# Last products of eight half groups by seven block products in an mLSTM cell with a multiplicative FFN

## The chip, the cores and the metric

The kernel runs on one core of a Trainium2 chip. A core has four computing engines that run side by side, each through its own queue of instructions: TensorE (PE in the profile; its weight loads are PEld), VectorE (DVE), ScalarE (ACT) and GpSimd (POOL). SyncE (SP) issues most DMAs, and ACT issues those of the output. [...]VectorE and ScalarE read PSUM, GpSimd works on SBUF.

The metric is the device time of one execution in microseconds (us); lower is better. All data are fp32.

## The reference

An mLSTM cell runs over 768 positions of 4 batches with 8 heads of 40. Its output, as 3072 tokens of 320 values, goes through a feed-forward block:

```python
for t in range(S):                                   # cell, per batch and head
    m_new = max(f_gate[t] + m, i_gate[t])
    f_stab, i_stab = exp(f_gate[t] + m - m_new), exp(i_gate[t] - m_new)
    C = f_stab * C + i_stab * outer(v[t], k[t])
    n = f_stab * n + i_stab * k[t]
    y[t] = sigmoid(o_gate[t]) * (C @ q[t]) / max(|n . q[t]|, 1)
x = y.transpose(0, 2, 1, 3).reshape(3072, 320)
a, b = x @ w1, x @ w2                                # 320 x 1024 each
out = ((a * b) @ w3) @ w_out                         # 1024 x 1024, 1024 x 320
```

## The kernel before

The two last weights are first multiplied into one, `w3o` (1024 x 320, eight blocks of 128 rows), so that out = (a * b) @ w3o. What is left is a cell and two products: the *up* products, which give a and b, and the *last* products.

**Steps.** One loop over 32 steps, `s` = 0 to 31 (L820), holds everything. The cell is cut into 24 pieces (`NU`) of one batch and 128 positions. Step `s` sends piece `s` through its first half (scores, state) and piece `s - 1` through its second half (`h`, denominators, `y`): this is "the cell's work", `quarter_work` (L338). Its PSUM is two tiles, `cell[0]` and `cell[1]`, of two banks each: `cell[0]` holds scores and state updates, `cell[1]` the two parts of `h`. The other four banks come from `mps` in turn. After step 24 the cell's banks are given to `mps` as well.

Four pieces of the same positions, one for each batch, make a group `gr` of 512 tokens; there are six. A half group `(gr, j)` has 256 tokens. `y` goes through DRAM (`send`, `get_back`) and comes back to be turned by VectorE (`x_turn`, L468), two steps after its piece.

**Up products.** Groups 0 to 2 use ordinary products (`up`), in steps up to 15. Groups 3 to 5 go by Strassen's scheme in Winograd's form, seven block products for eight (`up_by_seven`, L668), one eighth of a group's features each in steps 19 to 30. Its four parts are called in this order: `single` (three products into `pa` and `pb`, four `mps` banks), `shared` (four products for each of a and b into the cell's banks up to step 24: `p15` in `cell[1]`, copied out by ACT at L702 and L704, `p67` in `cell[0]`, added by VectorE at L684 and L686, then two adds by GpSimd at L711), `left` (the rest of the features on TensorE, and four adds that read `pa`, `pb` and the results of L711: "the left adds") and `product` (a * b on GpSimd, L729). The sums of tokens that the scheme needs are made by `token_sums` (L661), at the end of steps 17, 21 and 25.

**Last products.** Up to step 24 they are plain: `ffn_out` (L733) multiplies one block of 128 tokens with `w3o` in eight matmuls of 320 columns, into the cell's banks; ACT copies the result out and issues the DMA. `downs` lists 14 blocks, groups 0 to 2 and the first half of group 3; `n_down` says how many a step takes: two in steps 16 to 20, one in steps 21 to 24.

The five half groups from (3, 1) on go by seven (`out_by_seven`, L772), each 28 matmuls of 160 columns, at steps 27, 29 and three at step 31 (`n_out`). They need four sums of quarters of `w3o` (`out_weight_sums`, L748: one at step 24 and three at step 25, on GpSimd) and four sums of quarters of a * b (`ab_sums`, L763: on VectorE). In what follows A11 to A22 are the quarters of a half group of a * b, S1 to S4 their sums, B11 to B22 the quarters of `w3o`, T1 to T4 their sums.

**Order.** TensorE's instructions keep the order in which the program has them (`in_order`, L84), and so do those of every other engine (`keep_order`, L549, called in the last step for the whole loop, L979). Between the engines semaphores are set where data or memory ask for it. In a step the order is: `single` and `shared`, the last products, `left`, the cell's work; then, with GpSimd first, `product`, sums of output weights, `ab_sums` (at step 25 here, else at the end of the block), `x_turn`, the transposes of the next keys and queries (`turn`), `token_sums`; then `weighted`, `weights`, `masks` for the next piece (GpSimd L330, ACT L303, GpSimd L308), and the loads of later pieces. After step 24, `single` comes behind the last products.

Of the kernel before, what the change touches and what calls it, by code (L numbers as in the profile page):

```python
# [8 lines left out]
FP = mybir.dt.float32  # L9
U32 = mybir.dt.uint32  # L10
AF = mybir.ActivationFunctionType
OP = mybir.AluOpType
# [4 lines left out]
def kernel(  # L17
# [49 lines left out]
    io = ctx.enter_context(tc.tile_pool(name="io", bufs=3))  # L67
# [23 lines left out]
    def mm(out, lhsT, rhs, start=True, stop=True):  # L91
        in_order(nc.tensor.matmul(out, lhsT=lhsT, rhs=rhs, start=start, stop=stop))  # L92
# [134 lines left out]
        pend.append((dst, raw_tile(dst.shape[-1] if dst is not None else CW, pieces), i, part))  # L227


    w3T_t = {}  # L230
    turned_w3, ready_w3 = [], []

# [4 lines left out]
    def convert():  # L237
        if not scaled:
            scale_next()
        dst, raw, ko, half = scaled.pop(0)  # L240
        if dst is not None:
            to_f32(dst, raw)
            return
        w3 = wst.tile([128, CW], FP, name="w3", tag="w3")
        to_f32(w3, raw)
        if half == 0:
            w3T_t[ko] = wst.tile([128, FO, 128], FP, name="w3T", tag="w3T")
        nc.vector.transpose(out=w3T_t[ko].rearrange("c k (m r) -> c m k r", r=32)[:, 2 * half:2 * half + 2],
                            in_=w3.rearrange("r (m c k) -> r m k c", m=2, k=FO))
        if half:  # L250
            turned_w3.append(ko)
# [495 lines left out]

    def out_weight_sums():  # L748

        T_o.extend(m[:, i * KH * NH:(i + 1) * KH * NH].rearrange("p (f n) -> p f n", n=NH)  # L750
                   for m, i in ((v_all, 0), (gates, 0), (gates, 1), (q_all, 0)))
        (B11, B12), (B21, B22) = ([w3o[:, k * KH:(k + 1) * KH, i * NH:(i + 1) * NH] for i in range(2)] for k in range(2))
        T1, T2, T3, T4 = T_o
        for dst, p, q in ((T1, B12, B11), (T2, B22, T1), (T3, B22, B12), (T4, B21, T2)):
            yield nc.gpsimd.tensor_tensor(out=dst, in0=p, in1=q, op=OP.subtract)

    T_o, S_o = [], {}
    wsums = out_weight_sums()

    def quarters_of_ab(gr, j):  # L760
        return [[ab_t[gr][j][:, k * KH:(k + 1) * KH, t * P:(t + 1) * P] for k in range(2)] for t in range(2)]

    def ab_sums(gr, j):  # L763
        mem = [t.rearrange("p h d -> p (h d)") if j == 0 else io.tile([P, H, L], FP, name="pw", tag="pw", bufs=5)
               .rearrange("p h t -> p (h t)") for t in kbuf]
# [6 lines left out]
    def out_by_seven(gr, j, sums=None):  # L772
# [6 lines left out]
        o2 = (v_all, q_all)[j][:, 2 * DM:4 * DM].rearrange("p (i n) -> p i n", n=NH)  # L779

        def products(pairs, name):
            po = mps([P, len(pairs), NH], name)
            for i, (a, b) in enumerate(pairs):
                for f in range(KH):
                    mm(po[:, i], a[:, f, :], b[:, f, :], start=(i == f == 0), stop=(i == len(pairs) - 1 and f == KH - 1))
            return po
# [6 lines left out]
        for i in range(2):  # L793
            nc.vector.tensor_tensor(out=o2[:, 1 + i], in0=p67[:, i], in1=o2[:, i], op=OP.add)
        nc.vector.tensor_tensor(out=o2[:, 1:4:2], in0=o2[:, 1:3], in1=o2[:, 3:4].to_broadcast([P, 2, NH]), op=OP.add)
        nc.vector.tensor_tensor(out=o2[:, 0:2], in0=p23, in1=o2[:, 0:2], op=OP.add)
        nc.vector.tensor_tensor(out=o2[:, 2:3], in0=p4, in1=o2[:, 2:3], op=OP.add)
# [6 lines left out]
    downs = [(gr, j) for gr in range(NG) for j in range(GT)][:14]  # L804
    outs = [(gr, j) for gr in range(3, NG) for j in range(2)][1:]
# [14 lines left out]
    for s in range(len(n_up)):  # L820
# [33 lines left out]
            ab_sums(*summed.pop(0))  # L854
        def pairs():
            for i in range(n_out[s]):
                out_by_seven(*outs.pop(0))
                if summed and n_out[s] > 1:
                    ab_sums(*summed.pop(0))

        seven = None
        if s == NU + 3:
            pairs()
        if n_seven[s]:
            seven = up_by_seven(*sevens.pop(0), (lambda i: cell[i // 2][:, i % 2].rearrange("p (i t) -> p i t", i=2)) if s <= NU else
                                lambda i: mps([128, 2, TH], "p67" if i < 2 else "p15"), nc.gpsimd if sevens else nc.vector)
# [5 lines left out]
        else:  # L872
            for _ in range(n_down[s]):
                ffn_out([downs.pop(0)])
        if s != NU + 3:
            pairs()
        if seven and s > NU:
            seven[0]()
        now = [ups.pop(0) for _ in range(n_up[s])]
# [132 lines left out]
```

## Time and profile before

| | us |
|---|---|
| three runs | 426.82, 427.91, 428.42 |
| median | 427.91 |
| the profiled execution's own time | 427.89 |
| its span in the trace | 425.84 |
| steps 21 to 23, each | 14.13 |
| from the end of the cell (335.03) to the end of TensorE's work (about 422.6) | 87.6 |

The span runs from the first instruction to the last; some 2 us of the execution lie around it. The granted TensorE clock was 0.996 of full speed over the whole span, and full in every stretch from 240 us on.

A busy time in the profile is a sum of durations. A matmul's duration includes the time in which it runs beside the next, so its cost is better read from the distance of two starts: the 56 instructions of a half group by seven take 7.61 from the first to the start of what follows, 0.136 each. One fp32 product stands as two instructions in the trace.

A bracket at the end of a timeline line says how long the engine sat idle before the line and what ended this.

### The profile page before, as it was taken

What the parts mean: (1) busy time and instruction counts of PE and PEld (TensorE: products, weight loads), DVE (VectorE), ACT (ScalarE), POOL (GpSimd) and SP (SyncE); (2) the same over time, 40 slices, a digit from 0 to 9 for tenths busy, and PEclk for the clock granted to TensorE, in tenths of its full rate; (3) what the DMA queues carried; (4) which work ended last, traced back from release to release, by engine and by line L of the source; (5) the groups of instructions that cost most, each with busy time, mean ns of one, the idle gap of its engine ahead of it and who ended that gap; (6) DMA issues with size and microseconds to landing.
All of it is one profiled execution on the core that took longest, in us unless ns stands there. A gap on an engine that the chain in (4) does not pass through costs nothing.

```text
span 425.8 us, 13079 instructions
## 1 busy us (share of the span) xinstructions
PE 414.1 (97%) x5353; PEld 335.3 (79%) x5353; DVE 313.5 (74%) x635; ACT 150.1 (35%) x404; POOL 154.3 (36%) x211
## 2 busy tenths in 40 slices
PE   7989989999999999999999999999999999999996
PEld 4768878888688788787777778788778879888896
DVE  6676986888949779778736966596868699575971
ACT  4766865567723623630433313032311110210000
POOL 4421342233303303303307751546453587542100
PEclk9989999999999999999999999999999999999999
DMA  8999998598977776985425675756421120000001
GB/s 186 204 173 245 214 144 140 134 193 180 215 183 154 166 182 135 181 164 105 89 80 130 153 141 121 142 133 117 87 44 36 35 39 2 31 2 31 2 32 62
DMA packets 135211, 51.15 MB, mean 120 GB/s; under 512 B 109360, under 2 KB 126960, under 8 KB 135152
## 3 DMA queue, kind: packets, MB, share of 16 engines
q1 hardware_dynamic: 131552, 46.29, 53.9%
q10 hardware_dynamic: 3600, 4.03, 2.7%
q8 instruction: 42, 0.69, 0.7%
q14 instruction: 17, 0.14, 0.1%
HBM read 44.50 MB, written 5.80 MB: 118 GB/s over the span
## 4 chain that ended last, share of the span: by engine, by line
PE 53%; issue 20%; DVE 7%; POOL 7%; SPq 7%; DMA 5%; ACT 1%; POOLq 0%; DVEq 0%
PE cell L92 17%; PE pa L92 12%; PE o L92 8%; PE pb L92 8%; PE p L92 3%; POOL pw L308 3%; SPq L184 3%; DVE w3T L666 2%; PE pt L95 1%; POOL vw L330 1%; SPq L148 1%; DMA raw<-in_moe_w_dram 1%; PE fill L92 1%; POOL raw L659 1%; POOL state L335 1%
## 5 line engine op out<-in xcount | busy, mean ns | idle before, releaser
L335 POOL TENSOR_TENSOR state<-state,decay 128x164 f32<-128x164 f32 x40 | 20.0, 500 | 154.8 <-DVE state L404 129.0
L92 PE MATMUL pa<-xT,w 128*128 128x256 f32 x240 | 60.4, 382 | 0.0
L92 PEld LDWEIGHTS pa<-xT,w 128*128 128x128 f32 x240 | 44.4, 190 | 6.8 <-DVE h L430 0.4
L303 ACT ACTIVATE pw<-pw,aT 128x64 f32<-128x64 f32 x184 | 46.4, 339 | 3.2 <-ACT o_sb L741 1.9
L92 PE MATMUL pb<-xT,w 128*128 128x256 f32 x192 | 45.4, 379 | 0.0
L729 POOL TENSOR_TENSOR ab<-ab,a_sb 128x512 f32<-128x512 f32 x22 | 29.4, 1356 | 32.2 <-DVE ab L684 32.2
L92 PEld LDWEIGHTS pb<-xT,w 128*128 128x128 f32 x192 | 36.4, 190 | 5.0
L711 POOL TENSOR_TENSOR wo<-wo 128x512 f32<-128x512 f32 x22 | 27.4, 1268 | 29.8 <-DVE wo L686 29.8
L92 PE MATMUL pa<-xT,wr 64*64 64x256 f32 x384 | 37.0, 386 | 0.5 <-DVE wr L200 0.5
L92 PE MATMUL wp<-wo,w3T 128*128 128x320 f32 x128 | 35.9, 433 | 1.1 <-DVE ab L639 0.6
L308 POOL TENSOR_SCALAR_AFFINE_SELECT pw<-pw 64x512 f32<-64x512 f32 x48 | 35.8, 746 | 3.0 <-ACT pw L303 1.2
L92 PE MATMUL pb<-xT,wr 64*64 64x256 f32 x384 | 36.4, 380 | 0.0
L92 PE MATMUL cell<-w3o,ab 128*128 128x320 f32 x128 | 35.4, 432 | 0.0
L638 ACT ACTIVATE a_sb<-pa 128x512 f32<-128x512 f32 x24 | 14.3, 598 | 59.0 <-PE pb L92 59.0
L639 DVE TENSOR_TENSOR ab<-pb,a_sb 128x512 f32<-128x512 f32 x24 | 16.4, 688 | 23.2 <-ACT a_sb L638 22.8
L92 PEld LDWEIGHTS wp<-wo,w3T 128*128 128x128 f32 x128 | 23.8, 190 | 10.5 <-DVE ab L639 0.8
L92 PEld LDWEIGHTS cell<-w3o,ab 128*128 128x128 f32 x128 | 24.3, 190 | 9.5
L92 PEld LDWEIGHTS pa<-xT,wr 64*64 64x64 f32 x384 | 18.9, 132 | 15.4 <-issue 8.8
L686 DVE SCALAR_TENSOR_TENSOR a_sb<-pa,wo 128x512 f32<-128x512 f32 x12 | 8.3, 689 | 29.8 <-PE pa L92 29.8
L430 DVE TENSOR_TENSOR h<-cell,h 64x164 f32<-64x164 f32 x88 | 28.6, 326 | 1.6
L92 PE MATMUL po<-w3o,ab 128*128 128x320 f32 x96 | 26.4, 433 | 0.0
L92 PEld LDWEIGHTS po<-w3o,ab 128*128 128x128 f32 x96 | 18.1, 190 | 7.3
(180 smaller groups left out, 846.4 us busy)
## 6 DMA issues: line engine op xcount, KB each, us to landing
raw<-in_moe_w_dram SPq DMA_DIRECT2D x64, 128.0 KB, 3.4
kbuf<-in_k_dram SPq DMA_DIRECT2D x24, 160.0 KB, 4.5
v_all<-in_v_dram SPq DMA_DIRECT2D x24, 160.0 KB, 4.9
o_in<-in_o_gate_dram SPq DMA_DIRECT2D x24, 160.0 KB, 4.8
pw<-U_d SPq DMA_DIRECT2D x28, 128.0 KB, 3.5
raw<-in_moe_w_dram SPq DMA_DIRECT2D x5, 512.0 KB, 6.7
raw<-in_moe_w_out_dram SPq DMA_DIRECT2D x8, 320.0 KB, 4.1
gates<-in_k_dram SPq DMA_DIRECT2D x28, 80.0 KB, 2.5
```

Source lines behind the costliest of these rows:

```text
L92: in_order(nc.tensor.matmul(out, lhsT=lhsT, rhs=rhs, start=start, stop=stop))
L184: nc.sync.dma_start(out=dst, in_=src)
L303: nc.scalar.activation(out=pw[:, h, :], in_=src[:, h, :], func=AF.Exp, bias=aT[:, c, b * H + h:b * H + h + 1])
L308: nc.gpsimd.affine_select(out=pw[r], in_=pw[r], compare_op=OP.is_ge, fill=0.0, base=0, pattern=[[0, H], [1, L]], channel_multiplier=-1)
L335: nc.gpsimd.tensor_tensor(out=new, in0=old, op=OP.mult, in1=decay[:, b * NP:(b + 1) * NP, 2 * c + x:2 * c + x + 1] .to_broadcast([P, NP, D1]))
L430: nc.vector.tensor_tensor(out=part, in0=ph[x][halves[e]], in1=part, op=OP.add)
L638: nc.scalar.mul(out=a_sb, in_=pa, mul=UP ** -2)
L639: nc.vector.tensor_tensor(out=ab_t[gr][j][:, fs[0]:fs[-1] + 1, t0:t0 + a_sb.shape[-1]], in0=pb, in1=a_sb, op=OP.mult)
L666: nc.vector.tensor_tensor(out=dst, in0=p, in1=q, op=OP.subtract)
L686: nc.vector.scalar_tensor_tensor(out=out, in0=p, scalar=UP ** -2, in1=q, op0=OP.mult, op1=OP.add)
L711: aside_by.tensor_tensor(out=kept[j][:, 1:4:2], in0=kept[j][:, 1:3], in1=kept[j][:, 3:4].to_broadcast([128, 2, TH]), op=OP.add)
L729: aside_by.tensor_tensor(out=t[:, f:FO:FH, :], in0=t[:, f:FO:FH, :], in1=a, op=OP.mult)
```

## The change

- The last products of all half groups from (2, 0) on, eight in place of five, go by seven. The six blocks of group 2 and the first half of group 3 leave `downs`. `n_out` puts one half group into each of steps 21, 22, 24, 26 and 28, and three into step 31; `n_down` takes two blocks in steps 16 to 18 and one in steps 19 and 20.
- Up to step 24 the seven products go into the cell's four banks: `o15` and `o23` into `cell[1]`, `o67` and `o4` into `cell[0]`. Later they use `mps`, as before.
- The order of the products is A11 B11, A12 B21, S1 T1, (copy by ACT), S4 B22, S2 T2, S3 T3, A22 T4. Six adds in place of five follow on VectorE.
- The sums of output weights are made at steps 19 (T1, T2, T4) and 20 (T3). T1, T2 and T4 lie in a tile of the pool `ab`; T3 is written over B12.
- `ab_sums` stands at the end of the step before its half group, ahead of `x_turn`, for all but the last three. For groups below 4, S3 and S4 are made by GpSimd. The sums of (2, 0), (2, 1) and (3, 0) share one more tile of the pool `ab`.
- The two buffers `w3` of the weight conversion become halves of one tile, `w3_m`, which then holds the results of (2, 0), (2, 1) and (3, 0) until their DMA.
- The half group of step 27, which stood ahead of the up products, has no place of its own any more; last products always follow `shared`.

```diff
-        w3 = wst.tile([128, CW], FP, name="w3", tag="w3")
+        w3 = w3_m[:, half * CW:(half + 1) * CW]
...
     def out_weight_sums():
-        T_o.extend(m[:, i * KH * NH:(i + 1) * KH * NH].rearrange("p (f n) -> p f n", n=NH)
-                   for m, i in ((v_all, 0), (gates, 0), (gates, 1), (q_all, 0)))
+        mem = ffn.tile([128, FO, TH], FP, name="ab", tag="ab", bufs=6).rearrange("p f t -> p (f t)")
+        T_o.extend(mem[:, i * KH * NH:(i + 1) * KH * NH].rearrange("p (f n) -> p f n", n=NH) for i in range(3))
+        T_o.insert(2, B12)
         T1, T2, T3, T4 = T_o
-        for dst, p, q in ((T1, B12, B11), (T2, B22, T1), (T3, B22, B12), (T4, B21, T2)):
+        for dst, p, q in ((T1, B12, B11), (T2, B22, T1), (T4, B21, T2), (T3, B22, B12)):
             yield nc.gpsimd.tensor_tensor(out=dst, in0=p, in1=q, op=OP.subtract)
...
     def ab_sums(gr, j):
+        if not S_o:
+            S_m.append(ffn.tile([128, FO, TH], FP, name="ab", tag="ab", bufs=6).rearrange("p f t -> p (f t)"))
+        mem = [S_m[0][:, i * KH * P:(i + 1) * KH * P] for i in range(4)] if gr == 2 or (gr, j) == (3, 0) else [
...
-            nc.vector.tensor_tensor(out=dst, in0=p, in1=q, op=op)
+            by = nc.gpsimd if gr < 4 and (dst is S3 or dst is S4) else nc.vector
+            by.tensor_tensor(out=dst, in0=p, in1=q, op=op)
...
-        p15 = products(((A11, B11), (S1, T1)), "o15")
-        nc.scalar.copy(out=o2[:, 0:4:3], in_=p15)
-        p67 = products(((S2, T2), (S3, T3)), "o67")
-        p23 = products(((A12, B21), (S4, B22)), "o23")
-        p4 = products(((A22, T4),), "o4")
+        p15, p23, p67, p4 = (bank[i][:, 0:n] if bank else mps([P, n, NH], name)
+                             for i, (n, name) in enumerate(((2, "o15"), (2, "o23"), (2, "o67"), (1, "o4"))))
+        product(p15, 0, A11, B11)
+        product(p23, 0, A12, B21)
+        product(p15, 1, S1, T1)
+        nc.scalar.copy(out=o2[:, 2:4], in_=p15)
+        product(p23, 1, S4, B22)
+        product(p67, 0, S2, T2)
+        product(p67, 1, S3, T3)
+        product(p4, 0, A22, T4)
+        add(slice(0, 2), p23, slice(2, 4))
+        add(2, p67[:, 0], 2)
+        add(1, o2[:, 1], 2)
+        add(2, p67[:, 1], 2)
+        add(3, o2[:, 3], 2)
+        add(2, p4[:, 0], 2)
...
-    n_down = [0] * 16 + [2] * 5 + [1] * 4 + [0] * 7
-    n_out = [0] * 27 + [1, 0, 1, 0, 3]
+    n_down = [0] * 16 + [2] * 3 + [1] * 2 + [0] * 11
+    n_out = [0] * 21 + [1, 1, 0, 1, 0, 1, 0, 1, 0, 0, 3]
...
-        if s == NU + 3:
-            pairs()
...
-            for _ in range({NU: 1, NU + 1: 3}.get(s, 0)):
+            for _ in range({19: 3, 20: 1}.get(s, 0)):
                 next(wsums)
-            if s == NU + 1:
+            if s < len(n_up) - 2 and n_out[s + 1]:
                 ab_sums(*summed.pop(0))
...
-            if s < len(n_up) - 2 and n_out[s + 1] and s > NU + 2:
-                ab_sums(*summed.pop(0))
```

More of the change, by code (lines that the diff above doesn't have):

```diff
@@ L227, in fetch @@
         pend.append((dst, raw_tile(dst.shape[-1] if dst is not None else CW, pieces), i, part))
+    w3_m = wst.tile([128, 2 * CW], FP, name="w3_m", tag="w3_m", bufs=1)
     w3T_t = {}
@@ L748, in out_weight_sums @@
     def out_weight_sums():
-        T_o.extend(m[:, i * KH * NH:(i + 1) * KH * NH].rearrange("p (f n) -> p f n", n=NH)
-                   for m, i in ((v_all, 0), (gates, 0), (gates, 1), (q_all, 0)))
+        mem = ffn.tile([128, FO, TH], FP, name="ab", tag="ab", bufs=6).rearrange("p f t -> p (f t)")
         (B11, B12), (B21, B22) = ([w3o[:, k * KH:(k + 1) * KH, i * NH:(i + 1) * NH] for i in range(2)] for k in range(2))
+        T_o.extend(mem[:, i * KH * NH:(i + 1) * KH * NH].rearrange("p (f n) -> p f n", n=NH) for i in range(3))
+        T_o.insert(2, B12)
         T1, T2, T3, T4 = T_o
-        for dst, p, q in ((T1, B12, B11), (T2, B22, T1), (T3, B22, B12), (T4, B21, T2)):
+        for dst, p, q in ((T1, B12, B11), (T2, B22, T1), (T4, B21, T2), (T3, B22, B12)):
             yield nc.gpsimd.tensor_tensor(out=dst, in0=p, in1=q, op=OP.subtract)
-    T_o, S_o = [], {}
+    T_o, S_o, S_m = [], {}, []
     wsums = out_weight_sums()
@@ L763, in ab_sums @@
     def ab_sums(gr, j):
-        mem = [t.rearrange("p h d -> p (h d)") if j == 0 else io.tile([P, H, L], FP, name="pw", tag="pw", bufs=5)
+        if not S_o:
+            S_m.append(ffn.tile([128, FO, TH], FP, name="ab", tag="ab", bufs=6).rearrange("p f t -> p (f t)"))
+        mem = [S_m[0][:, i * KH * P:(i + 1) * KH * P] for i in range(4)] if gr == 2 or (gr, j) == (3, 0) else [
+               t.rearrange("p h d -> p (h d)") if j == 0 else io.tile([P, H, L], FP, name="pw", tag="pw", bufs=5)
                .rearrange("p h t -> p (h t)") for t in kbuf]
@@ L769, in ab_sums, with out_by_seven @@
                               (S4, A12, S2, OP.subtract)):
-            nc.vector.tensor_tensor(out=dst, in0=p, in1=q, op=op)
-    def out_by_seven(gr, j, sums=None):
+            by = nc.gpsimd if gr < 4 and (dst is S3 or dst is S4) else nc.vector
+            by.tensor_tensor(out=dst, in0=p, in1=q, op=op)
+    def out_by_seven(gr, j, bank):
         (A11, A12), (A21, A22) = quarters_of_ab(gr, j)
@@ L778, in out_by_seven, with product, add @@
         T1, T2, T3, T4 = T_o
[L779 to L786, printed above, removed]
-        p15 = products(((A11, B11), (S1, T1)), "o15")
-        nc.scalar.copy(out=o2[:, 0:4:3], in_=p15)
-        p67 = products(((S2, T2), (S3, T3)), "o67")
-        p23 = products(((A12, B21), (S4, B22)), "o23")
-        p4 = products(((A22, T4),), "o4")
[L793 to L797, printed above, removed]
+        o2 = (w3_m[:, 0:2 * DM] if gr == 2 or (gr, j) == (3, 0) else (v_all, q_all)[j][:, 2 * DM:4 * DM]).rearrange("p (i n) -> p i n", n=NH)
+        p15, p23, p67, p4 = (bank[i][:, 0:n] if bank else mps([P, n, NH], name)
+                             for i, (n, name) in enumerate(((2, "o15"), (2, "o23"), (2, "o67"), (1, "o4"))))
+        def product(po, i, a, b):
+            for f in range(KH):
+                mm(po[:, i], a[:, f, :], b[:, f, :], start=(i == f == 0), stop=(i == po.shape[1] - 1 and f == KH - 1))
+        def add(i, p, q):
+            nc.vector.tensor_tensor(out=o2[:, i], in0=p, in1=o2[:, q], op=OP.add)
+        product(p15, 0, A11, B11)
[12 more added lines that the diff above has]
+        add(2, p4[:, 0], 2)
         for t in range(2):
@@ L803 @@
            for f in range(0, FO, 2)]
-    downs = [(gr, j) for gr in range(NG) for j in range(GT)][:14]
-    outs = [(gr, j) for gr in range(3, NG) for j in range(2)][1:]
+    downs = [(gr, j) for gr in range(2) for j in range(GT)]
+    outs = [(gr, j) for gr in range(2, NG) for j in range(2)]
     summed = list(outs)
@@ L856, in pairs @@
             for i in range(n_out[s]):
-                out_by_seven(*outs.pop(0))
+                out_by_seven(*outs.pop(0), [cell[x // 2][:, x % 2, 0:DM].rearrange("p (i n) -> p i n", n=NH) for x in (2, 3, 0, 1)]
+                             if s <= NU else [])
                 if summed and n_out[s] > 1:
@@ L874 @@
                 ffn_out([downs.pop(0)])
-        if s != NU + 3:
-            pairs()
+        pairs()
         if seven and s > NU:
```

## The prediction

> **What bounds the kernel now.** I read the page's first part, then the chain of waits from 250 us on, then the timelines of single engines around the steps that the change touches. TensorE is busy almost without a gap:
>
> ```profile
> PE 414.1 (97%) x5353; PEld 335.3 (79%) x5353; DVE 313.5 (74%) x635; ACT 150.1 (35%) x404; POOL 154.3 (36%) x211
> ```
>
> From 250 us on the chain is nearly all TensorE. One step of the loop (step 21) and two entries from other steps, each line start, length, what:
>
> ```profile
> 263.71 12.07 PE cell L92 x48
> ...
> 279.36 1.06 PE pa L92 x4
> 280.42 0.43 PE pb L92 x2
> 280.85 0.86 PE pa L92 x4
> 281.71 0.43 PE pb L92 x2
> 282.15 7.76 PE cell L92 x32
> 289.91 1.02 PE pa L92 x16
> 290.93 0.86 PE pb L92 x16
> 291.79 1.70 PE cell L92 x112
> ...
> 379.36 7.61 PE o L92 x56
> ```
>
> See here a price list. The single up-products take 2.79, the shared ones with one plain block 7.76, the rest of the up-products 1.88, the cell 1.70: 14.13 a step. Step 20 has two blocks and 12.07 for 7.76, so a block costs 4.31 and the shared products 3.45. A half group by seven is 7.61; as two plain blocks it is 8.62. A step with one block takes 14.13, with a half group 17.43, with neither 9.82.
>
> The other engines have their work behind this. DVE's left adds of a step begin 1.15 after TensorE's rest products (291.05 against 289.91) and end 0.3 after the cell; its h ends 0.5 before the next shared products want those banks (281.45, 281.98). So VectorE may come some 0.5 to 1.7 late for nothing; what is later stops TensorE. GpSimd at the end of step 19:
>
> ```profile
> 264.61 2.74 POOL L729 TENSOR_TENSOR ab<-ab,a_sb 128x512 f32<-128x512 f32 x2
> 267.31 0.99 POOL L330 TENSOR_TENSOR vw<-v_all,wT 128x328 f32<-128x328 f32 x1
> 268.25 1.38 POOL L308 TENSOR_SCALAR_AFFINE_SELECT pw<-pw 64x512 f32<-64x512 f32 x2
> 269.71 0.47 POOL L335 TENSOR_TENSOR state<-state,decay 128x164 f32<-128x164 f32 x1
> ...
> 338.14 1.54 POOL L755 TENSOR_TENSOR v_all<-w3o 128x640 f32<-128x640 f32 x1
> ```
>
> The first four follow without a gap and end at 270.18; then come the two L711 adds (2.49), whose result the left adds read. The last line, from step 24, is the price of a sum of output weights.
>
> How wide a wait on PSUM is shows in one copy, once from the two-bank tile cell, once from separate one-bank tiles p:
>
> ```profile
> 326.36 0.60 ACT L704 ACTIVATE wo<-cell 128x512 f32<-128x512 f32 x1 [6.84 <-PE cell L92]
> ...
> 368.68 0.60 ACT L704 ACTIVATE wo<-p 128x512 f32<-128x512 f32 x1 [5.38 <-PE p L92]
> ```
>
> Its products end 0.86 after the shared ones begin (324.38 and 367.51), so at 325.24 and 368.37. From p the copy starts 0.3 later. From cell it starts 1.1 later, when the products in the other bank have ended as well. A wait on cell covers both banks.
>
> [...]L443 takes 0.54 at 282.74 and 1.29 at 264.93 beside L729; L770 takes 0.68 alone and 1.35 to 2.02 at 345 to 352 beside GpSimd.[...]
>
> **Part by part.** Sums are against the profiled execution: 427.89, of which the span is 425.84. That is within 0.02 of the median of the runs.
>
> *Products.* Six plain blocks become three half groups: 3 x (8.62 - 7.61) = 3.0 saved on TensorE, the bound engine. Steps 19 and 20 become 14.13, step 21 and 22 17.43, 23 9.82, 24 16.6. After the cell the same five half groups remain. There TensorE took 87.6 from 335.03 to the end against 6 x 8.13 + 5 x 7.61 = 86.8. Some 0.6 of this is around the half group of step 27, whose sums run from 345.5 to 352.5 against GpSimd; half on GpSimd and one step earlier, I count 0.2 of it back. Gain 3.2.
>
> *Weight sums, step 19.* Put 0 at the end of step 19's cell (260.85 in the old trace). GpSimd ends L729 at +6.5, then three sums: the first behind L445 with 0.25, then 3 x 1.54, to +11.4; vw, masks and decay 2.58, to +13.9; L711 2.49, to +16.5. These sums stand before vw, masks and step 20's L711 in program order, which every engine but TensorE keeps. In a step with one block the second and the fourth left add stand at +12.6 and +13.8, and read the first and the second L711. The fourth can now only start at +16.6, and h, 2.46 after that start (278.99, 281.45), ends at +19.1. TensorE wants the h banks at 14.13 + 2.69 = +16.8. Stall 2.35. It contains the 1.0 for which the single products wait on the second left add. It would cost nothing if GpSimd had 4.9 us of air here; it has 0.8 idle before L711 and 1.2 between L711's end and the fourth add.
>
> *Step 21, half group (2,0).* Shared products end at +22.6. VectorE's y is late with h and shares with the fourth weight sum and S3 (y to +23.0); S1 and S2 0.65 each to +24.3, x_turn and two transposes 2.35, then the adds that read the shared p67, 0.8 per j, to +28.25. S4 on GpSimd is there at +25.6. Products: two without sums to +24.8, S1 by T1 to +25.9. Now ACT copies o15 out of cell: 0.2 to start, 0.43, then S4 by B22 goes on at +26.6, as it writes the other bank of the same tile: 0.7 lost. S2 by T2 writes cell[0], so it waits for both p67 adds: +28.3 in place of +27.7, 0.6 lost. With 2.35 this is 3.6.
>
> *Step 22, half group (2,1).* Now from the end of step 21's cell: the copy costs 0.7 again. VectorE: y +4.9, S1, S2 +6.2, x_turn and transposes +8.5, four token sums 1.45 alone, 4.7 in all at 238.22 beside GpSimd. Here the masks, pushed to +8.3 by S3 and S4, run beside them: 2.0 taken, bounds 1.45 and 3.2. p67 adds to +12.2, TensorE there at +11.2: 1.1 lost (0.5 to 2.0). Sum 1.8.
>
> *Steps 23 and 24.* No block covers VectorE in step 23: p67 adds end at +9.1 where the cell wants cell[0] at +8.9, 0.2. Left adds come 1.5 late, h with them: 0.75 at step 24's shared products. The copy in (3,0) 0.7. Sum 1.65.
>
> *At nothing.* Out adds: six for five on VectorE, half a microsecond late at the left adds, inside their slack. The w3_m staging: over 10 us between uses. The two output DMAs on ACT wait for the last add, and the exps queued behind them have a step of air. SP: send, loads and get_back are as many as before, in shorter steps; y of step 19 landed about 15 after the send was due, x_turn stands at +24.3: up to 1.3 late, counted only in the range. Two DMAs and a last add end the kernel as now.
>
> *Sum.* -3.2 + 3.6 + 1.8 + 1.65 = +3.85: 431.7.
>
> **Rivals.** Measurements of this kernel can tell about 0.5%, 2.1 us, from no change.
>
> A, faster: GpSimd's backlog does not reach TensorE. One place: step 20's L711. If the pair ended by +14.2 (sums begun before L729's end, or vw and masks cheaper), the 2.35 and most lateness behind it vanish, and step 23 has its air. Left: three copies, at most 2.0, part of it hidden in the gaps: 425.9. For it: GpSimd is busy only 36% of the span. Against: the unbroken row above, with 2.0 of air for 4.9 of sums.
>
> B, waits by single bank on a write after a read: no 3 x 0.7, p67 adds free 0.8 earlier twice, h 0.3 earlier: about 3.2 less, 428.5. For it: no line shows TensorE held by a read of the other bank. Against: the copy's wait above is by tile.
>
> C, lateness adds up: turned x comes 1.3 late at step 20, token sums take 3.2: 434.2.
>
> That a half group in cell's banks doesn't go at 0.136 a matmul is possible; the o rows show one price throughout, so I give it no share.
>
> **Numbers.** Chances: forecast 0.50, A 0.13, B 0.21, C 0.16. Range 427.6 to 434.4: it leaves out A and a part of B below, a little above. Faster by over 0.5% (below 425.75): most of A, 0.11. Within: B and a rest of A and of the forecast, 0.25. Slower: 0.64.
>
> **What would show it.** In the new trace: GpSimd's L755 x3 right behind L729 of step 19, then L711 ending 16.5 after step 19's cell; PE cell waiting for DVE h in step 21; gaps of 0.7 before the S4 products with ACT's copy as releaser in steps 21, 22 and 24 and none after step 24; S2 products waiting for L684. TensorE's 14.13, 17.43 and 9.82 plus these gaps give the steps. I am wrong if L711 ends early, if no gap follows the copy, or if the stretch after the cell is longer than 87.6.

## The result and the profile after

| | before | after |
|---|---|---|
| median of 8 runs each, on one chip | 427.03 (424.64 to 428.73) | 432.5 (431.25 to 435.54) |
| ratio, with its 95% interval | | 1.0141 (1.0101 to 1.0181) |
| profiled execution | 427.89 | 431.3 |
| span | 425.84 | 429.6 |

The change makes the kernel slower by 1.4%, which is 6.0 us of 427.03 (the medians alone lie 5.5 apart). The level, 432.5, is close to the 431.7 of the prediction, but part of this is luck: the forecast starts from 427.89, which is 0.9 above the median of the eight runs, and adds 3.85, which is too little. The two errors offset each other. The 3.4 between the two profiled executions looks like a hit and is not one: the execution profiled before had a stretch with half the TensorE clock near its start (granted clock 0.83 on the mean from 20 to 30 us and 0.50 from 24 to 26, so a third of it at half speed; 1.00 from 20 to 30 after the change). That is some 1.7 of TensorE's time which the other has not. So I compare from the start of step 19's single products: to the end of the span it is 184.1 before and 190.1 after. That is 6.0 again.

Step lengths, from one start of the single products to the next (steps 19 to 24), and what follows the cell:

| kernel | 19 | 20 | 21 | 22 | 23 | 24 | sum | behind the cell |
|---|---|---|---|---|---|---|---|---|
| before | 19.13 | 18.44 | 14.13 | 14.13 | 14.14 | 13.34 | 93.3 | 90.8 |
| after | 14.82 | 14.14 | 21.00 | 19.97 | 10.07 | 18.34 | 98.3 | 91.7 |

Of the 6.0, the steps give 5.0 and the stretch behind the cell 0.9.

The first part of the page, busy time and share of the span of each engine:

```profile
PE 412.1 (96%) x5425; PEld 339.1 (79%) x5425; DVE 321.2 (75%) x662; ACT 148.4 (35%) x401; POOL 163.6 (38%) x219
```

TensorE is busy for 2.0 less than before (414.1) and the kernel is slower. So the time lies in gaps. The table by stretch of the changed kernel shows where, for steps 21 and 22 (columns: stretch, its length, busy time and instructions of each engine, granted clock, DMA share, GB/s):

```profile
268.48:289.48 21.00, 18.73 (x232) 15.70 (x228) 16.26 (x34) 2.66 (x8) 13.76 (x13) 1.00 0.74 139
289.48:309.45 19.97, 17.94 (x233) 16.03 (x229) 16.30 (x37) 3.97 (x14) 10.03 (x10) 1.00 0.29 73
```

Before, TensorE was busy for 14.13 of 14.13 in both. The timeline of TensorE shows each gap:

```profile
270.42 0.70 PE L92 MATMUL pb<-xT,raw 128*128 128x256 f32 x2 [0.81 <-DVE a_sb L687]
...
273.43 0.70 PE L92 MATMUL cell<-xT,w 128*128 128x256 f32 x2 [0.85 <-DVE h L431]
...
279.36 1.25 PE L92 MATMUL cell<-ab 128*128 128x160 f32 x8
281.21 1.32 PE L92 MATMUL cell<-w3o,ab 128*128 128x160 f32 x8 [0.61 <-POOL pw L309]
282.44 1.35 PE L92 MATMUL cell<-ab 128*128 128x160 f32 x8
...
299.66 1.32 PE L92 MATMUL cell<-w3o,ab 128*128 128x160 f32 x8 [0.61 <-POOL pw L309]
302.41 1.35 PE L92 MATMUL cell<-ab 128*128 128x160 f32 x8 [1.42 <-DVE wo L685]
```

In the lines of the half groups x8 is one block product (four products, eight instructions) and x16 is two. Read it from the top. In step 21 the single products wait for the left adds, then the shared ones for h. In an undisturbed step the shared products start 2.70 after the single ones; here it is 4.95, so 2.25 is lost. Then, in both steps, there is a gap ahead of S4 by B22. Eight instructions take 1.09 from start to start; from 279.36 to 281.21 it is 1.85, so 0.76 is lost. In step 22 the next eight, S2 by T2, are late by another 1.66 (299.66 + 1.09 = 300.75, they start at 302.41). The name "POOL pw L309" need not be the cause of the 0.61: ScalarE's copy of o15 runs just there (`w_m` is `w3_m` without its number),

```profile
280.64 0.42 ACT L800 COPY w_m<-cell 128x320 f32<-128x320 f32 x1 [4.06 <-PE cell L92]
```

and it ends at 281.06, 0.06 before one of GpSimd's selects (L309) ends. The two experiments on the copy, e1 and e11, settle which of the two it is.

GpSimd's timeline of the changed kernel, at the end of step 19 and in step 20, is the counterpart of the unbroken lines shown of before:

```profile
258.11 2.75 POOL L730 TENSOR_TENSOR ab<-ab,a_sb 128x512 f32<-128x512 f32 x2
260.81 1.79 POOL L757 TENSOR_TENSOR ab<-w3o 128x640 f32<-128x640 f32 x1
262.68 3.17 POOL L757 TENSOR_TENSOR ab<-w3o,ab 128x640 f32<-128x640 f32 x2
265.80 0.74 POOL L331 TENSOR_TENSOR vw<-v_all,wT 128x328 f32<-128x328 f32 x1
266.49 1.38 POOL L309 TENSOR_SCALAR_AFFINE_SELECT pw<-pw 64x512 f32<-64x512 f32 x2
267.95 0.47 POOL L336 TENSOR_TENSOR state<-state,decay 128x164 f32<-128x164 f32 x1
268.37 2.49 POOL L712 TENSOR_TENSOR wo<-wo 128x512 f32<-128x512 f32 x2
```

The three weight sums (L757) stand behind the product and push all that follows. The adds whose result the left adds read (L712 now, L711 before) end at 270.86. Step 19's cell ended at 254.34: that is +16.5, the forecast number.

VectorE's timeline of the changed kernel, first in step 20, then in step 22:

```profile
263.19 0.58 DVE L473 STREAM_TRANSPOSE xT<-yb 128x384 f32<-128x384 f32 x1 [1.98 <-DMA yb<-y_d]
...
269.67 0.69 DVE L687 SCALAR_TENSOR_TENSOR a_sb<-pb,wo 128x512 f32<-128x512 f32 x1 [1.82 <-POOL wo L712]
...
298.42 0.63 DVE L667 TENSOR_TENSOR w3T<-xT 128x256 f32<-128x256 f32 x1
299.07 0.75 DVE L667 TENSOR_TENSOR w3T<-xT,w3T 128x256 f32<-128x256 f32 x1
299.75 0.68 DVE L667 TENSOR_TENSOR w3T<-xT 128x256 f32<-128x256 f32 x1
300.36 0.41 DVE L667 TENSOR_TENSOR w3T<-xT,w3T 128x256 f32<-128x256 f32 x1
300.69 0.87 DVE L687 SCALAR_TENSOR_TENSOR wo<-cell,wo 128x256 f32<-128x256 f32 x2
301.48 0.87 DVE L685 TENSOR_TENSOR wo<-cell,wo 128x256 f32<-128x256 f32 x2
```

In step 20 VectorE itself stands 1.98 in `x_turn`, waiting for y to come back from DRAM. It costs nothing there, because GpSimd holds the left adds up longer; keep it in mind. In step 22 the token sums take 2.35 (298.42 to 300.77), and the adds that read p67 stand behind them.

Behind the cell, TensorE's and GpSimd's timelines of the changed kernel around the half group of step 26:

```profile
349.55 2.34 PE L92 MATMUL o<-w3o,ab 128*128 128x160 f32 x16
351.72 1.25 PE L92 MATMUL o<-ab,pw 128*128 128x160 f32 x8
353.64 1.35 PE L92 MATMUL o<-w3o,pw 128*128 128x160 f32 x8 [0.67 <-POOL pw L776]
```

```profile
347.55 2.95 POOL L730 TENSOR_TENSOR ab<-ab,a_sb 128x512 f32<-128x512 f32 x2 [0.82 <-DVE ab L685]
350.46 1.71 POOL L776 TENSOR_TENSOR pw<-ab 128x512 f32<-128x512 f32 x1
352.14 1.44 POOL L776 TENSOR_TENSOR pw<-ab,pw 128x512 f32<-128x512 f32 x1
```

Here S4 by B22 waits for S4 itself, the second of the two sums that went to GpSimd. They queue behind the product (L730). This half group takes 8.54 from start to start (349.55 to 358.09) in place of 7.61.

### The profile page after: what moved, and what is told of

Same layout as the page of the kernel before. It is cut to its first block, busy times and chain, and to the rows that moved or that the text cites. A ratio compares the mean times of both kernels' runs of the same rounds, so it can differ in the third digit from the quotient of the medians.

```text
span 429.6 us, 13242 instructions
## 1 busy us (share of the span) xinstructions
PE 412.1 (96%) x5425; PEld 339.1 (79%) x5425; DVE 321.2 (75%) x662; ACT 148.4 (35%) x401; POOL 163.6 (38%) x219
## 4 chain that ended last, share of the span: by engine, by line
PE 72%; DVE 13%; POOL 6%; issue 4%; DMA 2%; ACT 1%; SPq 0%; DVEq 0%; POOLq 0%; ACTq 0%
PE pa L92 19%; PE pb L92 13%; PE cell L92 12%; PE wp L92 8%; PE o L92 8%; PE p L92 4%; PE po L92 4%; POOL ab L730 2%; PE px L95 2%; DVE h L431 2%; PE pt L95 1%; DVE w3T L667 1%; DVE ab L685 1%; DVE pw L398 1%; POOL ab L757 1%
## 5 line engine op out<-in xcount | busy, mean ns | idle before, releaser
L730 POOL TENSOR_TENSOR ab<-ab,a_sb 128x512 f32<-128x512 f32 x22 | 29.1, 1341 | 39.5 <-DVE ab L685 39.5
L309 POOL TENSOR_SCALAR_AFFINE_SELECT pw<-pw 64x512 f32<-64x512 f32 x48 | 35.8, 746 | 1.6
L712 POOL TENSOR_TENSOR wo<-wo 128x512 f32<-128x512 f32 x22 | 27.5, 1270 | 16.1 <-DVE wo L687 16.1
L92 PE MATMUL cell<-w3o,ab 128*128 128x160 f32 (+1 forms) x128 | 23.7, 334 | 1.8 <-POOL pw L309 1.2
L92 PEld LDWEIGHTS cell<-w3o,ab 128*128 128x128 f32 x128 | 19.7, 190 | 4.9 <-POOL pw L309 1.6
L92 PEld LDWEIGHTS pb<-xT,wr 64*64 64x64 f32 x384 | 20.1, 133 | 3.0
```

Of the source, the lines that this page charges most:

```text
L309: nc.gpsimd.affine_select(out=pw[r], in_=pw[r], compare_op=OP.is_ge, fill=0.0, base=0, pattern=[[0, H], [1, L]], channel_multiplier=-1)
L712: aside_by.tensor_tensor(out=kept[j][:, 1:4:2], in0=kept[j][:, 1:3], in1=kept[j][:, 3:4].to_broadcast([128, 2, TH]), op=OP.add)
L730: aside_by.tensor_tensor(out=t[:, f:FO:FH, :], in0=t[:, f:FO:FH, :], in1=a, op=OP.mult)
```

## The experiments

The theory after the first look at both traces was the prediction's, with the sizes just read: a stall of 2.3 from the weight sums, three gaps of 0.76 from the copy, 1.7 from the token sums, 1.3 behind the cell. The main rival was that VectorE and GpSimd are simply full in steps 20 to 22, so that what is removed in one place comes back in the next. Each of the experiments e1 to e5 undoes one part. This table has the steps of all of them:

| kernel | 19 | 20 | 21 | 22 | 23 | 24 | sum | behind the cell | ratio to before |
|---|---|---|---|---|---|---|---|---|---|
| e1 copy later | 14.83 | 14.16 | 21.11 | 21.65 | 10.06 | 17.49 | 99.3 | 91.7 | 1.0166 (1.0118 to 1.0213) |
| e2 weight sums | 14.83 | 14.84 | 19.76 | 19.98 | 10.11 | 18.35 | 97.9 | 91.7 | 1.0173 (1.0120 to 1.0225) |
| e3 S3, S4 on VectorE | 14.83 | 14.64 | 22.06 | 20.41 | 10.08 | 18.29 | 100.3 | 90.8 | 1.0211 (1.0167 to 1.0255) |
| e4 token sums | 14.89 | 14.13 | 21.09 | 18.28 | 10.08 | 18.34 | 96.8 | 91.7 | 1.0099 (1.0068 to 1.0129) |
| e5 after the cell | 14.84 | 14.14 | 20.99 | 19.98 | 10.12 | 18.35 | 98.4 | 90.3 | 1.0109 (1.0052 to 1.0166) |
| e6 four edits | 14.83 | 14.14 | 22.97 | 17.66 | 10.43 | 17.49 | 97.5 | 90.3 | 1.0105 (1.0060 to 1.0150) |
| e7 old order | 14.82 | 14.14 | 25.07 | 24.59 | 10.14 | 18.28 | 107.0 | 90.3 | 1.0275 (1.0235 to 1.0315) |
| e8 transposes | 14.83 | 14.14 | 19.61 | 17.44 | 10.68 | 17.51 | 94.2 | 90.3 | 1.0020 (0.9999 to 1.0040) |
| e10 turned x | 14.82 | 14.13 | 17.68 | 17.43 | 10.75 | 17.49 | 92.3 | 90.3 | 0.9957 (0.9938 to 0.9977) |
| e11 copy ahead | 14.82 | 14.13 | 18.28 | 18.28 | 10.08 | 18.34 | 93.9 | 90.3 | 0.9987 (0.9964 to 1.0010) |

Steps are from one profiled execution each and repeat within about 0.1 where nothing was changed. For differences of about 1 us they tell more than the ratios of e1 to e7, which rest on four runs each (seven for e4) and have intervals of 0.6 to 1.1%.

### e1: the copy behind S4 by B22

```diff
-        nc.scalar.copy(out=o2[:, 2:4], in_=p15)
         product(p23, 1, S4, B22)
+        nc.scalar.copy(out=o2[:, 2:4], in_=p15)
```

> The changed kernel with ACT's copy of o15 moved behind the product S4 by B22. Theory (a wait on the two-bank tile cell holds TensorE during the copy): the three gaps of 0.76 us ahead of S4 by B22 in steps 21, 22 and 24 are gone. In steps 21 and 22 S2 by T2 then comes earlier to its own wait for the p67 adds, which end as before, so most of the 0.76 comes back there: the span falls by 0.8 to 1.0 us (step 24 and a remnant of step 21), from 429.6 to about 428.7. Rival 1 (the gap is S4 coming late from GpSimd): no gap moves, span unchanged. Rival 2 (the gaps simply add up): the span falls by 2.3 us.

Median 433.4, no gain: the span was to fall by 0.8 to 1.0, and the steps take 1.0 more. TensorE's timeline of this kernel, steps 21 and 22:

```profile
283.17 1.35 PE L92 MATMUL cell<-ab 128*128 128x160 f32 x8 [0.78 <-DVE wo L685]
...
303.14 2.16 PE L92 MATMUL cell<-ab 128*128 128x160 f32 x8 [2.27 <-DVE wo L685]
```

The gap ahead of S4 by B22 is gone, although L309 was not moved: the copy made it, and the trace had named the other of two waits that end close together. But in both steps the same time comes back one block product later, as a wait for the p67 adds. Only step 24, where these adds are early, became shorter, by 0.84. And in step 22 two waits of 0.6 and 1.4 became one of 2.27, which had a price of its own. The table by stretch of this kernel:

```profile
303.10:305.10 2.00, 1.96 (x9) 1.96 (x10) 0.38 (x1) 0.00 (x0) 1.83 (x2) 0.61 0.03 8
305.10:307.10 2.00, 2.00 (x10) 2.00 (x10) 0.00 (x0) 0.00 (x0) 0.00 (x0) 0.54 0.00 0
307.10:309.10 2.00, 2.00 (x26) 1.64 (x28) 0.65 (x3) 0.00 (x0) 0.00 (x0) 1.00 0.00 0
```

The granted clock falls to a half after the wait (0.50 from 304 to 306) and comes back. Half speed over 3.4 costs 1.7, and step 22 is 1.68 longer than in the changed kernel.

### e2: three weight sums on VectorE, two of them a step earlier

```diff
...
-            yield nc.gpsimd.tensor_tensor(out=dst, in0=p, in1=q, op=OP.subtract)
+            yield (nc.gpsimd if dst is T3 else nc.vector).tensor_tensor(out=dst, in0=p, in1=q, op=OP.subtract)
...
-            for _ in range({19: 3, 20: 1}.get(s, 0)):
+            for _ in range({18: 2, 19: 1, 20: 1}.get(s, 0)):
```

> The changed kernel with T1, T2 (step 18) and T4 (step 19) made by VectorE, where it waits for turned x; T3 stays on GpSimd. Theory (three sums on GpSimd delay step 20's L712, this delays the left adds and h): L712 ends about 3.2 us earlier against the cell's end, the stall at step 21's single and shared products falls from 2.3 to about 0.4 us, total about 1.9 us less than the changed kernel. Rival (VectorE is full, lateness of x or of the sums takes the place): the left adds of step 20 are as late as now and less than 0.7 us is won.

The sum of the steps falls by 0.5 only, where 1.9 was expected: the rival's value. GpSimd's backlog is gone (L712 now waits for VectorE), and the other thing that was late in step 20 decides. VectorE's and TensorE's timelines of this kernel:

```profile
263.79 0.58 DVE L473 STREAM_TRANSPOSE xT<-yb 128x384 f32<-128x384 f32 x1 [1.64 <-DMA yb<-y_d]
```

```profile
267.92 0.69 PE L92 MATMUL cell<-qT,kT 40*64 40x64 f32 x32 [0.49 <-DVE wo L685]
272.29 0.70 PE L92 MATMUL cell<-xT,w 128*128 128x256 f32 x2 [0.58 <-DVE h L431]
```

VectorE stands in `x_turn` for the DMA, the p67 adds are queued behind it, and their lateness now reaches TensorE at the scores (0.49) and again at h. In the changed kernel the two delays lay beside each other. Steps 19 and 20 of the changed kernel are 4.3 shorter each, and y does not come back from DRAM as much sooner: VectorE waits 1.64 for it here, where in the kernel before the same transpose (267.63) followed without a wait.

### e3: S3 and S4 of all half groups on VectorE

```diff
-            by = nc.gpsimd if gr < 4 and (dst is S3 or dst is S4) else nc.vector
-            by.tensor_tensor(out=dst, in0=p, in1=q, op=op)
+            nc.vector.tensor_tensor(out=dst, in0=p, in1=q, op=op)
```

> The changed kernel with S3 and S4 of all half groups on VectorE. Theory (VectorE's chain sets the end of the p67 adds): step 21 1.3 longer, step 22 some 0.4 longer (the token sums then run beside less GpSimd work), step 24 the same, step 26 1.1 shorter since S4 no longer waits behind GpSimd's products: about 0.6 us more, 190.7 from step 19 on. Rival ([...]GpSimd's part slows VectorE as much as it relieves it): 189 or less.

The p67 adds come later in steps 21 and 22 (1.81 and 2.19 are lost between starts in place of 0.14 and 1.66), step 20 is 0.5 longer too, and the stretch behind the cell is 0.9 shorter, as S4 of step 26 no longer waits behind GpSimd's product. From step 19 on it is 191.1, where 190.7 was expected. So "half on GpSimd" helps where VectorE is late and harms behind the cell. The first effect is the larger one.

### e4: token sums behind the p67 adds

```diff
             seven[1]()
+            if s == 22:
+                token_sums(4)
...
-            if s - 2 in range(4 * GT - 1, NU, GT):
+            if s in (17, 25):
```

> The changed kernel with the token sums of group 4 moved from the end of step 21 to step 22, behind the adds of p67. Theory (token sums, slowed beside GpSimd, delay the p67 adds that S2 by T2 waits for): the wait of 1.7 us ahead of S2 by T2 in step 22 is gone, about 1.6 us less than the changed kernel. Rival (the lateness is that of h and y, not of the token sums): the p67 adds end less than 1 us earlier and under 0.7 us is won; or the token sums now delay the left adds of step 22 and the gain turns up as a wait in step 23.

Step 22 goes from 19.97 to 18.28, as expected, and the rest stays within 0.1. The wait of 1.66 was the token sums' and nothing takes its place.

### e5: from step 26 on, products, copy and adds in the order of before

```diff
+        if bank:
...
+        else:
+            nc.scalar.copy(out=o2[:, 0:4:3], in_=p15)
+            product(p67, 0, S2, T2)
+            product(p67, 1, S3, T3)
+            product(p23, 1, S4, B22)
+            product(p4, 0, A22, T4)
...
```

> The changed kernel; only where the products use banks of their own (from step 26 on) S2 by T2 and S3 by T3 stand ahead of S4 by B22, with the copy and the five adds of the kernel before. Theory (S4 of (3, 1) comes late from GpSimd; at the very end four adds follow the p67 products where one product is left to cover them): the half group of step 26 takes 7.7 us in place of 8.7, and VectorE's last add ends 0.35 us after TensorE in place of 0.75: 1.4 us less than the changed kernel. Rival (the delay in step 26 is in S1 or in banks): no change there and 0.4 us less in all.

The stretch behind the cell falls from 91.7 to 90.3, as expected. TensorE's timeline of this kernel, the half group of step 26:

```profile
349.14 2.34 PE L92 MATMUL o<-w3o,ab 128*128 128x160 f32 x16
...
356.75 0.59 PE L92 MATMUL pa<-xT,w 128*128 128x256 f32 x2
```

It takes 7.61 now, because S4 is asked for sixteen instructions later. The other part is the very end. In the changed kernel the last add ends at 426.65, 0.78 after TensorE's last product (425.87), since five adds follow S3 by T3 with one block product to cover them; in the kernel before it was 0.36 (422.95 against 422.59).

### e6: e1, e2, e4 and e5 together

> The changed kernel with all four edits tried so far (copy of o15 behind S4 by B22; T1, T2, T4 on VectorE in steps 18 and 19; token sums of group 4 behind the p67 adds of step 22; S2 by T2 and S3 by T3 ahead of S4 by B22 from step 26 on). Counted from the start of step 19's single products to the end of the span, before took 184.1, the changed kernel 190.1. Theory (TensorE waits on the p67 adds, which follow a VectorE chain that is late from step 19 on; the copy's gap only shows where those adds are early): 1.6 for the token sums, 1.3 for the order after the cell, 0.5 for the weight sums, 0.8 for the copy in step 24 and about 0.6 in step 22, nothing in step 21: 185.3, so still some 1.2 us slower than before. Rival (each edit's gap goes for good, copy 2.3 in all): 184.2.

From step 19 on it takes 187.9: better than the changed kernel, but 2.5 behind the expectation. Its VectorE and TensorE timelines:

```profile
282.78 0.58 DVE L473 STREAM_TRANSPOSE xT<-yb 128x384 f32<-128x384 f32 x1 [2.36 <-DMA yb<-y_d]
```

```profile
286.80 1.82 PE L92 MATMUL cell<-ab 128*128 128x160 f32 x8 [3.15 <-DVE wo L685]
```

With the smaller waits gone, `x_turn` at the end of step 20 waits for its DMA, the two transposes and the p67 adds stand behind it, and TensorE waits 3.15 at one place. Then the clock is halved again for 3.4, from 287.5 on (granted clock 0.50 from 288 to 290), with TensorE at work: 1.7 of the 2.5.

### e7: the products in the order of before, everywhere

```diff
         product(p15, 0, A11, B11)
-        product(p23, 0, A12, B21)
         product(p15, 1, S1, T1)
...
         product(p67, 1, S3, T3)
+        product(p23, 0, A12, B21)
+        product(p23, 1, S4, B22)
         product(p4, 0, A22, T4)
```

> The changed kernel with the order of products, copy and adds of the kernel before (A11, S1, copy, S2, S3, A12, S4, A22). Theory (in the cell's banks S2 by T2 waits for the p67 adds, and what stands ahead of it is its cover): in steps 21 and 22 five products in place of three follow the end of the p67 adds, 2.2 us more each; step 24 about 0.5 less, the steps after the cell 1.4 less: 2.4 us more than the changed kernel, 192.5 from step 19 on; if the longer idle halves TensorE's clock as in e1_copy_later, up to 195.9. Rival (the order is indifferent or better, as the copy's gap goes): 190 or less.

S2 by T2, which writes the banks that the p67 adds read, now comes 2.2 earlier. This kernel takes 197.4 from step 19 on, more than the 195.9 that was the most expected. TensorE's timeline of this kernel:

```profile
282.87 1.35 PE L92 MATMUL cell<-ab 128*128 128x160 f32 x8 [2.90 <-DVE wo L685]
...
307.02 2.50 PE L92 MATMUL cell<-ab 128*128 128x160 f32 x8 [4.54 <-DVE wo L685]
```

So the new order of the products is worth 8.7 in the steps of the changed kernel. Part of it is the clock. The table by stretch of this kernel, in four stretches of 1 us:

```profile
284.00:285.00 1.00, 1.00 (x6) 1.00 (x5) 0.00 (x0) 0.00 (x0) 1.00 (x2) 0.55 0.43 66
287.00:288.00 1.00, 1.00 (x7) 1.00 (x7) 0.00 (x0) 0.00 (x0) 0.00 (x0) 0.74 1.35 184
304.00:305.00 1.00, 0.00 (x0) 0.00 (x0) 1.00 (x3) 0.00 (x0) 0.69 (x2) 0.79 0.47 105
311.00:312.00 1.00, 1.00 (x8) 1.00 (x7) 0.00 (x0) 0.00 (x0) 0.00 (x0) 0.80 0.00 0
```

A mean of 0.55 says that the clock fell at 284.1, and 0.74 that it was back at 287.5; likewise 304.6 and 311.4. In between it is 0.50 (285 to 287 and 305 to 311). TensorE was at work through all of the first slow stretch and from 307.02 on in the second, so half speed cost 1.7 and 2.2. The other 4.8 is the waiting.

### e8: e6, and transposes out of the way of the p67 adds

```diff
+            if s in (21, 22):
+                turn(s)
...
-            if NY <= s - 2 < NU:
+            if NY <= s - 2 < NU and s not in (18, 19):
                 x_turn(s - 2)
...
-            if N_DVE <= s + 1 < NU:
+            if N_DVE <= s + 1 < NU and s not in (20, 21):
                 gated = turn(s + 1)
+            if s in (18, 19):
+                x_turn(s - 2)
```

The first lines stand behind `shared`, and so behind the p67 adds.

> As e6_four_edits, and VectorE's order changed: x_turn of steps 18 and 19 behind the transposes of keys and queries, and the transposes that ended steps 20 and 21 moved behind the p67 adds of the next step. Theory (the chain in front of the p67 adds is what TensorE waits for; in the long steps VectorE is idle after them): no wait over 0.3 us is left in steps 20 to 22, the stretch from step 19 on takes 182.0 to 183.0, 1 to 2 us less than before, ratio about 0.996. Rival (the work moved behind the adds is late at the left adds and the waits come back one step later, or the keys come late for the scores): 184.5 or more, no faster than before.

The kernel is now level with the one before. Its 184.5 from the start of step 19's single products is the rival's value, though not for the rival's reason: the turned x at the end of step 20, which was not moved, still stands ahead of the p67 adds, and there a wait is left. VectorE and TensorE in step 21:

```profile
278.36 0.58 DVE L473 STREAM_TRANSPOSE xT<-yb 128x384 f32<-128x384 f32 x1 [3.02 <-DMA yb<-y_d]
```

```profile
280.55 1.35 PE L92 MATMUL cell<-ab 128*128 128x160 f32 x8 [1.92 <-DVE wo L685]
```

### e10: the turned x of step 20 behind the p67 adds too

```diff
             if s in (21, 22):
                 turn(s)
+            if s == 21:
+                x_turn(18)
+                get_back(19)
...
-        if NY <= s - 2 < NU:
+        if NY <= s - 2 < NU and s != 21:
             get_back(s - 2)
...
-            if NY <= s - 2 < NU and s not in (18, 19):
+            if NY <= s - 2 < NU and s not in (18, 19, 20):
                 x_turn(s - 2)
```

> e8_transposes_later with one more move: x_turn(18) leaves the end of step 20 and stands in step 21 behind the p67 adds and turn(21), and the DMA that fetches the next turned x follows it. Theory (the 1.92 us left in step 21 of e8 is VectorE standing in x_turn(18), 3.02 us, for the DMA yb<-y_d, with the p67 adds queued behind it): that wait goes and no other takes its place, because the p67 adds are then ready about 3 us earlier than TensorE asks; step 21 takes 17.5 to 17.9 us instead of 19.61, steps 22 to 24 stay at 17.44, 10.68, 17.51 within 0.3, and from the start of step 19's single products to the end 182.6 to 183.3 us instead of 184.6: 0.8 to 1.5 us less than the kernel before (184.1), ratio 0.996 to 0.999. Rival (VectorE's queue is full in this step, so the wait only moves to the copy, the left adds or h): step 21 still over 19 us or step 22 over 18.5, 184 us or more.

As expected: step 21 takes 17.68 and nothing else moves. Median 424.18, in the comparison with 426.11 for the kernel before. The table by stretch of this kernel, steps 21 and 22:

```profile
268.60:286.30 17.70, 17.70 (x233) 15.83 (x228) 15.09 (x33) 2.70 (x8) 11.48 (x12) 1.00 0.65 132
286.30:303.70 17.40, 17.40 (x232) 15.99 (x228) 16.40 (x35) 3.16 (x10) 10.07 (x10) 1.00 0.55 112
```

TensorE is busy without a gap, at full clock, while VectorE is busy for 94% of step 22. It can be that full and be on time, so the main rival falls for these steps.

### e11: e10 with the copy ahead of S4 by B22 again

> e10_turned_x_after_adds with the copy of o15 back ahead of S4·B22, as in the changed kernel. Theory (the copy reads the tile of both halves of a cell bank pair, so that S4·B22 waits for it although it writes another bank): with nothing else late the gap of 0.75 to 0.8 us is back in steps 21, 22 and 24, and the three steps take 2.2 to 2.4 us more than in e10. Rival (what e1 showed holds here too: the gap is cover for a wait that comes later, so the sum changes by less): under 1.2 us in the three steps.

Steps 21, 22 and 24 become 0.60, 0.85 and 0.85 longer, together 2.3. TensorE's timeline of this kernel:

```profile
279.82 1.33 PE L92 MATMUL cell<-w3o,ab 128*128 128x160 f32 x8 [0.61 <-ACT w_m L802]
...
298.10 1.32 PE L92 MATMUL cell<-w3o,ab 128*128 128x160 f32 x8 [0.61 <-ACT w_m L802]
```

With the p67 adds early the copy's gap is a pure loss, and the trace now names the copy. Step 23 gets 0.67 of it back, since h comes early there; so the whole is 1.6 in the trace and 1.2 between the medians. In e1 the same gap was cover for a later wait, and taking it away gave nothing.

## Why the prediction was right, and where it was off

**The mechanism.** The forecast case (0.50) is what happened: L712 ends at +16.5, the left adds and h follow, the copy makes a gap in steps 21, 22 and 24, the token sums delay the p67 adds in step 22. Two things it said would be seen were not: the trace names ACT's copy as releaser in step 24 alone, and a gap ahead of S4 by B22 came after step 24 too, from S4 itself. "B, waits by single bank" is refuted by e10 against e11: only the copy's place differs, and S4 by B22 waits for a copy from the other bank of its tile. "A, GpSimd's backlog absorbed" falls by the wait for `a_sb L687` and h in step 21.

**"Step 21: with 2.35 this is 3.6".** Measured 3.57 over the counted 17.43: 2.25 at the single and shared products, 0.76 from the copy, 0.14 in place of 0.6 at the p67 adds. The other 0.4 is short delays that the prediction does not count: 0.2 where the shared products turn to `cell[0]`, and 0.1 each after the wait for h and at S2 by T2. That the weight sums cause the 2.25 is read from GpSimd's unbroken row and VectorE's wait for L712. e2 takes the sums away and with them the wait for the left adds, but a wait for h stays, for another reason; that both causes have to go is shown by e10, where step 21 has no gap. No run moves `x_turn` and leaves the weight sums on GpSimd.

**"p67 adds to +12.2, TensorE there at +11.2: 1.1 lost. Sum 1.8".** This is the term in the steps that was most off: 2.5. TensorE was there at +11.3, as forecast, but the adds ended at +12.9. VectorE's transposes ended 0.4 later than I had them, and the token sums took 2.35 where I took 2.0 between the bounds 1.45 and 3.2. e4 shows that without them in the way nothing is left of this wait.

**"Steps 23 and 24 ... Sum 1.65".** 2.0: the waits at the scores of step 23 (0.2), for h (0.75 between starts) and for the copy (0.77) have the forecast sizes. The rest, 0.3, is spread: the shared products take 3.55 and 3.56 in steps 23 and 24 for the counted 3.45, and S4 by B22 1.16 for 1.09.

**The stalls together** are 8.1 where 7.05 was forecast, over steps in which the products' gain of 3.0 is already counted: 5.0 in place of 4.05. That the 3.0 is real is shown by e10, whose step 22 has no gap and takes the 17.43 counted.

**"Half on GpSimd and one step earlier, I count 0.2 of it back".** Wrong in sign, and one of the prediction's own signs of being wrong came true: TensorE needs 88.0 from the end of the cell in place of 87.6. I had seen that the sums of the old step 27 suffered beside GpSimd (up to 2.02 for 0.68), and took moving half of them to GpSimd for a relief. But these sums then queue behind its product, and the new order of products asks for S4 first. e5 changes the order and brings 7.61; e3 changes the engine. With either alone TensorE needs 87.1, so the earlier place by itself is worth 0.5, more than the 0.2 counted, and the half on GpSimd, with the new order, cost 0.9.

**"Two DMAs and a last add end the kernel as now".** Also wrong, by 0.42: I counted the number of adds and not how many of them follow the last but one block product. The place to look was the order of the adds in the diff, against the one block product that is left to cover them.

**The sum.** 8.1 - 3.0 + 0.9 = 6.0, where 7.05 - 3.0 - 0.2 = 3.85 was forecast. Both the stalls and the stretch behind the cell came out worse.

**Two readings of the prediction are loose.** The 0.54 of L443 at 282.74 is not alone: GpSimd's selects (L308, from 282.29 on) run beside it, so the trace shows the slowing beside L729 (1.29) and hardly any beside the selects: 0.54, against 0.49 at 339.98, where GpSimd is idle. And "every engine but TensorE" in the part on the weight sums is wrong for this program, which holds TensorE to its order too, by `in_order`; no sum rests on it.

**What the stall of 2.35 hid.** Its size was right, and yet taking the weight sums off GpSimd (e2) gave 0.5. Turned x was counted "up to 1.3 late, counted only in the range", for step 21; the wait was already there in step 20, with 1.98. Under the bigger delay it was free; without it, it was the next bound. The prediction named what is late first and did not ask what would be late next on the other engine. That is of no weight for the time of this change, but it decides what a repair needs.

**Could the change have paid?** Of 3.0 saved on TensorE, e10 keeps 1.0 in the steps and 0.5 behind the cell, with e1, e2, e4, e5 and the moves of e8 and e10; its interval, 0.9938 to 0.9977, lies below one. What is left of the loss is mostly in steps 23 (10.75 for 9.82: a wait of 0.33 for h and a delay of 0.3 at the scores) and 24 (a wait of 0.58 for h); no run removes it.

## What to carry to other kernels

When a step gets shorter because the bound engine has less to do, list what in that step keeps its length, DMA round trips above all (here VectorE waited 1.98 for y in the changed kernel and 3.02 in e8), and move the instruction that waits for it behind those that the bound engine waits for: in a queue kept in order, one early wait delays all (the 3.02 of e8 came out as 1.92 at TensorE). Undo edits one by one and also together: here two delays lay beside each other, so that each looked free while the other was there, and of the four repairs e1, e2, e4 and e5, two gave far less alone than their own cost. If a releaser's name doesn't fit the change, move the suspect alone and see whether the gap goes.

## What the runs showed of the hardware

In e1 one long wait of TensorE cost more than the two short ones that it took the place of: 0.61 and 1.42 in the changed kernel became 2.27, and step 22 is 1.68 longer. Idle times in the trace of 2.27 (e1), 3.15 (e6), 2.90 and 4.54 (e7) each came with half the clock (0.50), for 3.4 in the first three and 6.8 with the last; over the 2 us after 1.55 and 1.92 (e3) and 1.92 (e8) the clock was 1.00.

The length of one wait is not the whole measure. In the 3.4 ahead of each fall (the length of all these slow stretches but one) TensorE was idle for 2.27 (e1), 2.66 (e6), 2.17 and 2.10 (e7). But in the kernel before it was idle for only 1.19 in the 3.4 ahead of the fall at 23.4, and there too the clock was low for 3.4. What decides was not shown, and neither was why 1.92 was free in e3 and e8, so these runs do not tell whether a wait of that length is safe elsewhere.
